# Group 0's units let in eight chain steps apart instead of six, in a fused attention and mixture-of-experts kernel

## The chip, the cores and the metric

The kernel runs on one core of a Trainium2 chip. The time is the device time of one execution in microseconds, start to end; lower is better. A core has a matmul engine (PE, with its weight loads PEld), VectorE (DVE), ScalarE (ACT), GpSimd (POOL) and SyncE (SP), each with its own queue of instructions that it works through in order, and 16 DMA engines that move data.

## What is computed

First a linear attention with a complex decay, for 4 batches, 8 heads, 768 positions and a head size of 48; then, for each of the 3072 tokens of 384 values, one of 8 experts or none.

```python
mag = sqrt(a_re**2 + a_im**2)
scale = minimum(mag, 0.999) / (mag + 1e-6)        # normalizes the decay
for t in range(768):                               # per batch and head
    S_re, S_im = a * S (complex, by row) + outer(k[t], v[t])
    y[t] = q[t] @ S_re
x = y as tokens (3072, 384)
compute = x @ w_skip > 0
e = argmax(x @ w_gate);  g = softmax(x @ w_gate)[e]
out = x + g * (relu(x @ w1[e]) @ w2[e])            # where compute, else x
```

## The kernel before

The 768 positions are six chunks of 128, taken in three groups of two chunks (NG = 3). Attention is done by chunks: inside a chunk as masked products, and across chunks by a state carried on. For this the running product of the decays is needed.

For each group five kinds of work are written as Python generators, and a small planner (class Order) mixes them into one program by estimated costs; afterwards a scheduler of the framework may move instructions within each engine's queue, so that the final order on each engine is fixed before the kernel runs.

- The chain (`chain`, L379 on) makes the running product position by position on VectorE: a step is a multiplication (L412, tile X) and an addition (L421, tile W), each needing the one before. A group has 65 steps, in eight pieces of 8 (the last of 9), and there are 195 in all; `cpos` counts them.
- The gates (`gate`, L343 on) prepare the decays of a piece for the chain: L265, L271, L272 and L275 on ScalarE, L270, L274 and L361 on VectorE.
- The consumers (`consume`, L473 on) turn a finished piece into scaled keys and queries: nw (L484) and iw (L511) on VectorE, with a sum of squares on PE (L493, tile sw) whose logarithm and exponential (L500, L501) ScalarE makes and L503 to L508 on VectorE use. For group 1 the result is written to DRAM by POOL (L533, tile kq); for groups 0 and 2 it is transposed on PE (L574).
- The units (`unit`, L640 on) are the attention of one chunk c and one batch b: eight for a group, numbered here 0 to 7 as 4 (c mod 2) + b. The names carry c and b: at_1_3 is chunk 1, batch 3, unit 7 of group 0. `unit_at` puts the products pa (L631) on PE for the next unit; the unit masks them on VectorE (L653, tile at, two halves), multiplies the carried state by the decay (L667, tile RX, from chunk 1 on), and lets PE add (L678, L679, L698, tile ps) and form the output (L709 and L712, tile py); ScalarE copies it (L714, tile yT), PE turns it (L718, tile px), and L725, L726 copy that out. The values come by DMA into one of two tiles vt (L628). Group 1's units read their keys and queries back from DRAM (L544, tile nat) and transpose them on PE (L559, tile tu).
- The router (`route`, L791 on) chooses the experts of a chunk's tokens when its four units are done: some 20 small VectorE instructions with a product on PE (L824 to L827, tile pr) between them, which L858 and L840 on VectorE read, and four scatters by POOL to the expert tables (L782, tile xs).

The units of a group are started when its last piece is consumed, while the next group's chain runs. `units` (L747 on) lets a unit in only when the chain has come far enough, by the constant PACE (L49) that the change touches. Chain 2's pieces after its first are consumed once group 0's eight units are done.

After the attention come the experts: two layers of matmuls for each, on PE, with the weights split in two parts (L993, L994), L1061 and L1088 to L1090.

Of the kernel before, what the change touches and what calls it, by code (L numbers as in the profile page):

```python
# [19 lines left out]
B, H, S, D = 4, 8, 768, 48  # L20
# [3 lines left out]
HC = 64  # L24
NCH = S // C
NG = NCH // 2
# [19 lines left out]
CREDIT = 600.0  # L46
SLACK = 0.6
AHEAD = 2
PACE = 6  # L49
FILL = 4  # L50
LATE = 6

# [60 lines left out]
class Kern:  # L113
# [633 lines left out]
    def units(self, g):  # L747
        self.nat(2 * g, 0)
        self.nat(2 * g, 1)
        self.unit_at(2 * g, 0)  # L750
        for cc in range(2):
            c = 2 * g + cc
            while self.routes_done < c - 1:
                yield 0, 200
            if c > 0:
                yield from self.make_F(c - 1)
            if not self.last(c):
                self.lg = self.rt.tile([128, B, H // 2, E + 1], F32, name=f"lg_{c}", tag="lg", bufs=2)
            self.xa = self.rt.tile([128, B, XW], F32, name=f"xa_{c}", tag="xa", bufs=2)
            self.nc.gpsimd.tensor_copy(self.xa[:, :, DM], self.tok[:, :, c])  # L760
            for b in range(B):

                while self.cpos < min((g + 1) * (HC + 1) + (cc * B + b) * PACE, NG * (HC + 1)):
                    yield 0, 100
                yield from self.unit(c, b)
                self.units_done += 1
            if not self.last(c):
                self.routes.append((self.lg_t, self.route(c, self.lg, self.xa)))
# [542 lines left out]
```

## Time and profile before

| | us |
|---|---|
| median of 3 runs | 517.73 |
| lowest and highest run | 512.75, 518.37 |
| the profiled execution | 521.83 |
| its span, first to last instruction | 520.1 |

| engine | busy us | share of the span |
|---|---|---|
| PE | 417.1 | 80% |
| DVE | 410.2 | 79% |
| ACT | 304.9 | 59% |
| POOL | 91.1 | 18% |

Busy time counts instructions at work, not waits for semaphores; a busy PE is not a PE at its peak. PE's clock has two levels, 2.4 and 1.2 GHz; the granted clock is given as a share of the upper one, 0.902 over the span. A line of the profile such as "L274 ... [4.62 <-ACT t L272]" says that the engine had been idle for 4.62 us before the instruction and that ScalarE's L272 ended this. A share of busy time is a mean over stages with different limits, so the rows below are taken by stage.

### The profile page before, as it was taken

How to read it: one execution, taken by the hardware profiler on the slowest of the kernel's cores; microseconds unless marked ns; L12 is line 12 of the kernel's file. 1: busy time of each engine (PE TensorE's matmuls, PEld its weight loads, DVE VectorE, ACT ScalarE, POOL GpSimd, SP SyncE). 2: the span in 40 equal slices, each digit the busy share in tenths (PEclk: the TensorE clock that was granted, in tenths of full speed). 3: DMA queues.
4: the chain of work that ended last, by engine and by line, in shares of the span. 5: the costliest groups of instructions: out<-in, count | busy, mean ns of one | idle time of the engine just before them, and what ended most of it. 6: DMA issues, size and time to landing. Idle time of an engine off the chain costs nothing. (4 is left out here: it accounts for less than half of the span.)

```text
span 520.1 us, 10025 instructions
## 1 busy us (share of the span) xinstructions
PE 417.1 (80%) x3253; PEld 363.1 (70%) x3253; DVE 410.2 (79%) x1119; ACT 304.9 (59%) x690; POOL 91.1 (18%) x156
## 2 busy tenths in 40 slices
PE   0346543599998422899999999999999999999994
PEld 0234322389776311787878888998999999999994
DVE  4899989998998699788988956989658678666731
ACT  5778868746464655578887663443256546554720
POOL 4002011121122355000000030212301112201111
PEclk9967668599996855699999999999999999999998
DMA  5558876799888766767745225455777777667301
GB/s 95 113 112 181 192 176 138 161 215 205 195 206 229 179 175 161 169 139 169 170 124 122 65 76 166 122 159 142 244 212 226 236 251 231 196 208 248 118 21 28
DMA packets 160370, 85.50 MB, mean 164 GB/s; under 512 B 134491, under 2 KB 154300, under 8 KB 160311
## 3 DMA queue, kind: packets, MB, share of 16 engines
q1 hardware_dynamic: 153975, 70.51, 54.1%
q0 software_dynamic: 5248, 14.07, 9.7%
q8 instruction: 28, 0.46, 0.4%
q10 hardware_dynamic: 1088, 0.20, 0.2%
q14 instruction: 31, 0.25, 0.1%
HBM read 61.62 MB, written 25.01 MB: 167 GB/s over the span
## 5 line engine op out<-in xcount | busy, mean ns | idle before, releaser
L493 PE MATMUL sw<-ws,ident 128*128 128x384 f32 x84 | 42.3, 637 | 36.0 <-ACT ws L479 35.9
L412 DVE TENSOR_TENSOR X<-W,ain 128x192 f32<-128x192 f32 x192 | 67.9, 354 | 3.7 <-ACT ain L338 0.2
L994 DVE TENSOR_TENSOR l<-r,h 128x768 fp32r<-128x768 f32 (+1 forms) x56 | 59.5, 1067 | 12.1 <-ACT h L993 11.8
L1063 ACT ACTIVATE hh<-ph 128x240 fp32r<-128x240 f32 x64 | 23.7, 374 | 57.6 <-PE ph L1061 57.6
L993 ACT CAST h<-r 128x768 fp32r<-128x768 f32 (+1 forms) x56 | 51.7, 928 | 6.8 <-DMA r<-in_moe_w_dram 5.6
L493 PEld LDWEIGHTS sw<-ws,ident 128*128 128x128 f32 x84 | 18.7, 244 | 48.3 <-ACT ws L479 38.3
L421 DVE TENSOR_TENSOR W<-X 128x96 f32<-128x96 f32 x192 | 48.9, 254 | 3.6
L1061 PE MATMUL ph<-xh,l 128*128 128x240 f32 x192 | 51.1, 275 | 0.0
L1061 PE MATMUL ph<-xh,h 128*128 128x240 f32 x192 | 49.7, 275 | 0.6 <-issue 0.6
L1061 PE MATMUL ph<-xl,h 128*128 128x240 f32 x192 | 49.3, 276 | 0.1
L581 ACT COPY qk<-tp 96x256 f32<-96x256 f32 x128 | 40.1, 370 | 12.4 <-PE tp L574 12.3
L574 PE MATMUL tp<-ident,iw 128*96 128x128 f32 x128 | 23.4, 329 | 29.7 <-DVE iw L511 24.6
L709 PE MATMUL py<-at,vt 128*64 128x128 f32 x384 | 43.7, 287 | 2.0 <-DMA vt<-in_v_dram 2.0
L1088 PE MATMUL po<-h,hh 128*120 128x384 f32 x128 | 43.4, 339 | 0.3 <-ACT hh L1063 0.3
L1089 PE MATMUL po<-l,hh 128*120 128x384 f32 x128 | 43.1, 336 | 0.0
L653 DVE TENSOR_TENSOR at<-pa,mask 128x512 f32<-128x512 f32 x48 | 32.6, 685 | 11.8 <-PE pa L631 11.3
L1090 PE MATMUL po<-h,hl 128*120 128x384 f32 x128 | 41.0, 342 | 0.0
L574 PEld LDWEIGHTS tp<-ident,iw 128*96 128x96 f32 x128 | 17.6, 153 | 33.5 <-issue 10.1
L782 POOL DMA_INDIRECT xs<-xa,sl x24 | 27.9, 1164 | 72.3 <-DVE RX L664 17.4
L1064 DVE SCALAR_TENSOR_TENSOR hl<-ph,hh 128x240 fp32r<-128x240 f32 x64 | 25.5, 403 | 16.6 <-ACT hh L1063 16.5
L631 PE MATMUL pa<-qk 96*128 96x128 f32 x256 | 35.3, 283 | 2.0 <-DVE at L653 1.7
L1061 PEld LDWEIGHTS ph<-xh,l 128*128 128x128 f32 x192 | 36.3, 189 | 0.0
(235 smaller groups left out, 1080.4 us busy)
## 6 DMA issues: line engine op xcount, KB each, us to landing
r<-in_moe_w_dram SPq DMA_DIRECT2D x24, 512.0 KB, 5.2
r<-in_moe_w_dram SPq DMA_DIRECT2D x32, 384.0 KB, 4.0
nat<-kq SPq DMA_DIRECT2D x8, 768.0 KB, 5.6
kq<-nw POOLq DMA_DIRECT2D x24, 192.0 KB, 3.6
kq<-iw POOLq DMA_DIRECT2D x24, 192.0 KB, 2.9
vt<-in_v_dram SPq DMA_DIRECT2D x24, 192.0 KB, 3.0
out_dram<-xa SPq DMA_DIRECT2D x24, 192.0 KB, 3.2
ain<-in_a_im_dram SPq DMA_DIRECT2D x90, 48.0 KB, 2.6
```

The lines of the kernel that those rows point to most:

```text
L412: V.tensor_tensor(X, prev.unsqueeze(1).to_broadcast([128, 2, 2, D]), windows(ain[:, j]), ALU.mult)
L421: self.cins = V.tensor_tensor(W[:, j, ::-1], X[:, :, 0], X[:, :, 1], ALU.add).ins
L493: nc.tensor.matmul(sw, self.ident, ws[:, :, c], start=(c == 0), stop=(c == 1))
L574: nc.tensor.transpose(tp[:, jj], src[:, s * 4 + jj], self.ident)
L581: nc.scalar.copy(o, tp[:, :, :, cc].rearrange("p j s b -> p b s j"))
L709: PE.matmul(py[j * 64:j * 64 + 64, hp], vt_[:, 2 * hp + j], at[:, 2 * hp + j], start=True, stop=(c == 0))
L993: nc.scalar.copy(hi[:, ks], raw)
L994: nc.vector.tensor_tensor(lo[:, ks], raw, hi[:, ks], ALU.subtract)
L1061: pe = PE.matmul(ph, w[:, k, js], x[:, k], start=(n == 0), stop=(n == len(terms) - 1))
L1088: PE.matmul(po, hh[:, j, sl], w2h[:, j], start=(j == 0), stop=False)
L1089: PE.matmul(po, hh[:, j, sl], w2l[:, j], start=False, stop=False)
L1090: pe = PE.matmul(po, hl[:, j, sl], w2h[:, j], start=False, stop=(j == NF - 1))
```

## The change

PACE was one number, 6, and is now a number for each group, 8 for group 0 and 6 for groups 1 and 2. Unit n of group g may be written once the chain's count is at 65 (g + 1) + n PACE, at most 195. For group 0 that was 65, 71, 77, ... 107 and is 65, 73, 81, ... 121. Groups 1 and 2 keep 130, 136, ... 172 and 195.

```diff
-PACE = 6
+PACE = (8, 6, 6)
@@ units
-                while self.cpos < min((g + 1) * (HC + 1) + (cc * B + b) * PACE, NG * (HC + 1)):
+                while self.cpos < min((g + 1) * (HC + 1) + (cc * B + b) * PACE[g], NG * (HC + 1)):
                     yield 0, 100
                 yield from self.unit(c, b)
```

What this does to the queues is seen in three places. In VectorE's queue the masks of group 0's eight units stood behind 76, 78, 81, 85, 90, 97, 101 and 107 chain steps, and now stand behind 76, 78, 82, 89, 97, 105, 113 and 121.

The first place is PE's queue around the product of group 0's first route, pr_0 (tri and ones are constants of the count, oh the chosen experts). Before:

```order
L718 MATMUL px_1_1_1637<-wg_100,yT_1_1_1635 128x105 x4
L709 MATMUL py_1_2_1754<-at_1_2_1719,vt0_162 64x128 x2
L698 MATMUL ps_1_2_1740<-vt0_162,nat_1_2_1544 96x48 x8
L712 MATMUL py_1_2_1754<-qk_0_1_201,st0_164 64x128 x2
L709 MATMUL py_1_2_1754<-at_1_2_1719,vt0_162 64x128 x2
L712 MATMUL py_1_2_1754<-qk_0_1_201,st0_164 64x128 x2
L709 MATMUL py_1_2_1754<-at_1_2_1719,vt0_162 64x128
L824 LDWEIGHTS tri_75
L824 MATMUL pr_0_1707<-oh_0_1672,tri_75 128x32
```

The same queue in the changed kernel, up to the same product:

```order
L718 MATMUL px_1_0_1625<-wg_100,yT_1_0_1623 128x105 x4
L631 MATMUL pa_1_2_0_1728<-qk_0_1_201 128x128 x4
L709 MATMUL py_1_1_1752<-at_1_1_1706,vt1_163 64x128 x2
L824 LDWEIGHTS tri_75
L824 MATMUL pr_0_1685<-oh_0_1662,tri_75 128x32
```

The product stood behind five of the pieces of unit 6 (py_1_2, ps_1_2), and now stands behind one half of unit 6's pa and the first two products of unit 5.

The second place is ScalarE's queue around L271 and L272 of gate 15, the last gate of group 1 (t_15 is what VectorE's L274 reads). Before:

```order
L705 COPY T_1_3_1895<-ps_1_3_1883 96x384
L479 ACTIVATE ws_13_1960<-W_13_1860 128x768
L714 COPY yT_1_3_1914<-py_1_3_1897 128x512
L271 ACTIVATE sq_15_1943<-sq_15_1943,col_80 128x432
L272 ACTIVATE t_15_1944,acc_108<-sq_15_1943,col_80 128x432
```

In the changed kernel:

```order
L681 COPY st1_165<-ps_1_1_1738 96x8x48
L705 COPY T_1_1_1750<-ps_1_1_1738 96x384
L271 ACTIVATE sq_15_1827<-sq_15_1827,col_80 128x432
L714 COPY yT_1_1_1769<-py_1_1_1752 128x512
L272 ACTIVATE t_15_1828,acc_108<-sq_15_1827,col_80 128x432
```

The copy in front of L272 was unit 7's and is now unit 5's. VectorE's L274 of gate 15 stood behind chain step 115 and unit 7's RX behind 108; now L274 stands behind 113 and unit 5's RX behind 106.

The third place is POOL's queue at the end of group 1, with the stores of its last piece (nw_15, iw_15) and the scatters of group 0's second route (xa_1). Before:

```order
L782 DMA xs_117<-xa_1_1454,sl_1_2104 2048x386
L760 COPY xa_2_2341<-tok_98 128x4
L533 DMA kq1_119<-nw_15_2170 64x8x96
L533 DMA kq1_119<-nw_15_2170 64x768
L782 DMA xs_117<-xa_1_1454,sl_1_2104 2048x386 x2
L533 DMA kq1_119<-iw_15_2204 64x768
L533 DMA kq1_119<-iw_15_2204 64x8x96
L782 DMA xs_117<-xa_1_1454,sl_1_2104 2048x386
```

In the changed kernel:

```order
L533 DMA kq1_119<-nw_15_2115 64x8x96
L533 DMA kq1_119<-nw_15_2115 64x768
L533 DMA kq1_119<-iw_15_2189 64x768
L533 DMA kq1_119<-iw_15_2189 64x8x96
L782 DMA xs_117<-xa_1_1504,sl_1_2207 2048x386 x4
```

Three of the four scatters stood ahead of the last two stores, and now all four stand behind them. On VectorE the first small instruction of that second route (L802) stood behind chain step 118 and now stands behind 132; L511 of the last piece stood behind 135 and now behind 136; and the first mask of group 1 stood behind 146 and now behind 149.

## Rows read from the trace of the kernel before

**Rows 1.** Windows: length, busy us (x instructions) of PE, PEld, DVE, ACT, POOL, clock, DMA.

```profile
113.50:157.90 44.40, 41.13 (x361) 33.85 (x360) 41.75 (x113) 25.77 (x60) 9.67 (x17) 1.00 0.91 208
157.90:174.60 16.70, 16.70 (x125) 13.26 (x124) 9.80 (x31) 7.24 (x16) 4.80 (x7) 0.69 0.87 219
174.60:196.00 21.40, 3.90 (x14) 1.72 (x12) 21.02 (x73) 12.46 (x29) 9.31 (x16) 0.61 0.67 163
220.50:302.70 82.20, 82.20 (x715) 66.59 (x715) 71.17 (x191) 62.40 (x151) 2.41 (x5) 1.00 0.57 130
302.70:520.10 217.40, 207.55 (x1758) 200.47 (x1758) 147.01 (x405) 99.80 (x203) 39.10 (x41) 0.99 0.56 171
```

**Rows 2.** The same view for two stretches at the lower clock.

```profile
158.80:169.10 10.30, 10.30 (x60) 7.95 (x59) 8.09 (x27) 2.83 (x7) 2.41 (x4) 0.50 0.88 223
213.40:220.30 6.90, 6.90 (x40) 6.79 (x39) 3.90 (x8) 4.66 (x9) 0.00 (x0) 0.51 0.58 108
```

**Rows 3.** VectorE's waits, 100 to 225 us: us in total, times, longest.

```profile
DVE sq L274 <- ACT t L272: 4.6, 1, 4.6
...
DVE ohs L858 <- PE pr L825: 2.0, 1, 2.0
```

**Rows 4.** Timeline: start us, us, engine, line, operation, tiles, [idle before <-releaser].

```profile
157.76 0.44 PE L709 MATMUL py<-at,vt 128*64 128x128 f32 x4 [1.55 <-DMA vt<-in_v_dram]
...
162.18 0.21 PE L824 MATMUL pr<-oh,tri 128*128 128x32 bf16 x1
...
162.45 0.17 DVE L858 TENSOR_TENSOR ohs<-ohs,cnt 128x8 bf16<-128x8 bf16 x1 [2.04 <-PE pr L825]
...
172.61 0.59 ACT L714 COPY yT<-py 128x512 f32<-128x512 f32 x1 [0.54 <-PE py L712]
...
174.57 0.61 DVE L274 SCALAR_TENSOR_TENSOR sq<-sq,t 128x432 f32<-128x432 f32 x1 [4.62 <-ACT t L272]
```

**Rows 5.** Timeline at the start of group 1's units.

```profile
200.13 2.84 POOL L782 DMA_INDIRECT xs<-xa,sl  x1 [2.75 <-DMA xs<-xa,sl]
...
200.87 0.95 DVE L511 TENSOR_TENSOR iw<-inv,W 128x768 f32<-128x768 f32 x1
...
202.95 1.31 POOL L533 DMA_DIRECT2D kq<-iw  x2
...
213.06 1.57 PE L559 MATMUL tu<-ident,nat 128*96 128x128 f32 x8 [0.78 <-DMA nat<-kq]
...
220.49 0.69 DVE L653 TENSOR_TENSOR at<-pa,mask 128x512 f32<-128x512 f32 x1 [3.15 <-PE pa L631]
```

**Rows 6.** Lines, 113.5 to 157.9 us, DVE then PE: count | busy us, mean ns | idle.

```profile
L653 DVE TENSOR_TENSOR at<-pa,mask 128x512 f32<-128x512 f32 x12 | 8.0, 683 | 0.5 <-PE pa L631 0.5
L421 DVE TENSOR_TENSOR W<-X 128x96 f32<-128x96 f32 x29 | 7.4, 255 | 0.6
...
L667 DVE TENSOR_TENSOR RX<-T,F 96x768 f32<-96x768 f32 x4 | 3.8, 947 | 0.0
...
L631 PE MATMUL pa<-qk 96*128 96x128 f32 x90 | 12.1, 282 | 0.8 <-DVE at L653 0.7
L698 PE MATMUL ps<-vt,nat 128*96 128x48 f32 x80 | 7.6, 245 | 0.0
L709 PE MATMUL py<-at,vt 128*64 128x128 f32 x83 | 7.3, 279 | 2.0 <-DMA vt<-in_v_dram 2.0
L718 PE MATMUL px<-wg,yT 128*128 128x105 f32 x48 | 6.4, 276 | 0.3 <-ACT yT L714 0.3
L493 PE MATMUL sw<-ws,ident 128*128 128x384 f32 x16 | 6.1, 505 | 0.1
L712 PE MATMUL py<-qk,st 96*64 96x128 f32 x32 | 3.2, 278 | 0.0
L678 PE MATMUL ps<-RX,ident 96*96 96x384 f32 x6 | 2.5, 498 | 0.0
L679 PE MATMUL ps<-RX,perm 96*96 96x384 f32 x6 | 2.4, 485 | 0.0
```

## The prediction

> **What bounds the kernel now.** I read three things, in this order: where the time lies by stage, which engine is full in each, and what the full engine waits for. The stages come from the windows of busy time [rows 1]. From 220.5 us on the matmul engine is full: 82.20 us busy of 82.20 while group 1's units run, and 207.55 of 217.40 from there to the end, for group 2's units and the experts. Whatever makes the stretch from 220.5 us begin earlier moves the end by the same amount, since the PE queue after it holds the same work. Before it, VectorE sets the pace: it is busy 41.75 us of 44.40 while group 1's chain and six of group 0's units run together, and 21.02 of 21.40 at the end of that chain. Between the two lies the stretch to look at, 157.9 to 174.6 us: VectorE is busy 9.80 us of 16.70. That is the tail of group 0's units, and the change touches exactly these.
>
> The waits of VectorE between 100 and 225 us [rows 3] name what it stood for: 4.6 us for ScalarE's `t`, and 2.0 us for the router's PE product `pr`. The timeline [rows 4] shows how the first two came about. PE idled 1.55 us for `vt` and began again at 157.76; from 158.8 to 169.1 us its granted clock was 0.50, the lower of its two levels, 1.2 GHz [rows 2]. Units 6 and 7 (the last two of group 0's eight, counted from 0) stand close behind each other in PE's queue, so everything behind them was late: `pr` at 162.18 behind the products of unit 6, for which L858 waited 2.04 us, and unit 7's `py`, for whose copy `yT` at 172.61 ScalarE waited with the gate's L271 and L272 behind it, so that VectorE's L274 began only at 174.57, 4.62 us late. The chain's own steps stand behind L858 and L274 on VectorE and waited too.
>
> **The change, part by part.** No instruction is added or removed but for the grouping of a few; units move. By VectorE's order the masks of units 2 to 7, which stood behind chain steps 81, 85, 90, 97, 101 and 107, now stand behind 82, 89, 97, 105, 113 and 121. Units 0 and 1 stay at 76 and 78, because they are admitted late.
>
> *Router's product.* PE's order has `pr` behind unit 6's `pa` and unit 5's first two products instead of behind half of unit 6's `py`. Its wait, 2.0 us, goes: -2.0.
>
> *Gate's chain on ScalarE.* The copy that stands in front of L272 of gate 15 is now unit 5's, whose multiplication RX is issued seven chain steps earlier than L274, not unit 7's. -4.6.
>
> *What is late next.* Does a unit fit between two masks eight steps apart? VectorE first: in 44.4 us it did 29 steps, and in the same stretch 8.0 us of masks and 3.8 us of RX [rows 6]; without these (44.4 - 11.8) / 29 = 1.12 us a step with the gates and consumption it carries, so eight steps and one unit (2 x 0.683 + 0.947 = 2.3) take 9.0 + 2.3 = 11.3 us. PE: one unit of the second chunk has 16 records of L631, L698, L709 and L712, 8 of L718, 2 each of L678 and L679, and 4 of the consumption's L493. By busy time over count [rows 6] that is 2.15 + 1.52 + 1.41 + 1.60 + 1.07 + 0.83 + 0.80 + 1.53 = 10.9 us; these lines overlap (47.6 us summed against 41.13 as a union), so 10.9 x 0.864 = 9.4 us. It fits at 2.4 GHz with 1.9 us to spare, and not at 1.2 GHz, where it would take 18.8. One low stretch like that of [rows 2], 10.3 us, loses 5.15 us of PE work; 1.9 are spare, so up to 3.3 us reach VectorE. With the four units of the second chunk the new waits lie between 0 and 4 x 3.3 = 13.2 us. I take 2.0, about the smaller of the two old waits once, since PE is no longer queued two units deep and the masks, the consumption's products and RX are in PE's order in the order in which VectorE needs them: +2.0.
>
> *Start of group 1.* Its units read `nat` from DRAM, which needs the last stores `kq<-iw` of chunk 15. Before, POOL's queue has three of the four scatters of the second route ahead of these: L511 began at 200.87 and ended near 201.8, but the stores were issued at 202.95, when the scatter of 200.13 was through its 2.84 us [rows 5]. Now all four scatters stand behind the stores: -1.1. The second route itself moves from step 118 to step 132; its last six small instructions move behind L511, but one chain step more stands before it, so L511 sees no difference that I can price. PE's first product of group 1 waited for `nat` until 213.06 and VectorE's first mask for PE until 220.49 [rows 5], so it is `nat` that starts the full stretch. The mask's 3.15 us of waiting is PE's lateness seen from VectorE and is not counted a second time: the order puts three chain steps more ahead of that mask, which uses the time without making PE earlier. From 213.4 to 220.3 PE ran at 0.51 [rows 2]; if that goes, half of 6.9 us, 3.4, is gained; I leave it where it is, since PE still idles between unit 7 and group 1.
>
> *What hides nothing more.* The gates, loads and consumption that move with the units lie beside VectorE's chain as before. DMA engines are at 0.91 busy while the units run six apart [rows 1]; spreading them cannot raise that.
>
> **Sum.** -2.0 - 4.6 - 1.1 + 2.0 = -5.7 us. The profiled execution took 521.83 us in all (span 520.1), which makes 516.1. The median of the three runs is 517.73, 0.8% under the profiled one; against it the same difference makes 512.0.
>
> The trace has PE's clock at 0.61 where the units have ended and PE has 3.90 us of work in 21.40, at 1.00 over the 44.4 us in which units stand six apart [rows 1], and falling right after an idle of 1.55 us [rows 2, 4]; by these rows a spacing of eight with 9.4 us of work in 11.3 lies nearer to the second, and the sum stays 516.1. The Trainium skill, page "TensorE: Matmul & The Clock Gate", section "HAM oscillation — how this bites in real kernels", says that a matmul engine whose short bursts are parted by waits is throttled again in every round. By that rule spreading the units is the wrong direction and every unit of the second chunk would run low, which gives 523.2. The trace agrees with it at 158.8 us and no run shown here has the spacing of eight. As a mechanism of this kernel it is the second rival below.
>
> **Rivals.**
> 1. *The waits come back elsewhere.* In two of the four spacings the clock falls and VectorE waits 3.3 us at L503 or L274: -7.7 + 6.6 = -1.1, 516.6. For it: L503 stands only three to four steps behind the mask that its product L493 follows on PE. Against: at 2.4 GHz that path fits.
> 2. *Slower: every unit of the second chunk runs low.* The place is PE between masks 97 and 121. Price 4 x 3.3 = 13.2 against 7.7: +5.5, 523.2. It decides from the third low spacing on (9.9 against 7.7). For it: 1.9 us of idle per spacing could lie in one piece, and an idle of 1.55 was enough once. Against: a low PE is full, and PE rose again after a full stretch.
> 3. *More than forecast.* No new wait, and group 1 starts at 2.4 GHz: -7.7 - 3.4 = -11.1, 506.6.
> 4. *The change does nothing.* Excluded by the order: six of eight units move.
>
> **How the numbers follow.** Forecast 0.45, rival 1 0.33, rival 2 0.12, rival 3 0.10. The predicted time is the forecast's, 512.0. The range reaches down to rival 3, 506.6, and up to three low spacings, -7.7 + 9.9 = +2.2, 519.9; beyond it stay rival 2's full price and a little below. About 1%, 5.2 us, is what a measurement of this kernel can tell from no change. The forecast lies just beyond it: most of its share and all of rival 3 are faster, the rest of it and rival 1 lie within, and of rival 2 most is slower. That makes 0.48, 0.41, 0.11.
>
> **What would show it.** Right: in the profile of the changed kernel VectorE's waits at L858 and at gate 15's L274 are gone, no wait of over 2 us stands between masks 3 and 7, the store of chunk 15's `iw` follows L511 at once, the masks of group 1 begin some 5 us earlier, and everything from there is shifted alike. Wrong: a granted clock of 0.5 through most of the second chunk's units with waits at L503, L274 or L653, or a stretch from group 1's first product to chain 2's end longer than before by what was won.

## The result, and the profile after

The changed kernel is slower, by little: 519.0 us (median of 20 executions, 517.27 to 523.05) against 516.83 us of before (20 executions on the same chip, 512.75 to 519.95). The ratio is 1.0055, with a 95% interval from 1.0034 to 1.0077. The forecast was 512.0 us. The time lies in the range that was given (506.6 to 519.9), near its upper end, and on the other side of no change.

The profiled execution of the changed kernel took 519.52 us (span 517.8), so it is 2.3 us *shorter* than the profiled one of before (521.83 us), while the median is 2.2 us longer. That is the first thing to see: one execution beside one execution gives the wrong sign here.

| | before | changed |
|---|---|---|
| median of 20, us | 516.83 | 519.0 |
| shortest of 20, us | 512.75 | 517.27 |
| profiled execution, us | 521.83 | 519.52 |
| its span, us | 520.1 | 517.8 |
| its granted clock, mean | 0.90 | 0.91 |

Windows of busy time of the changed kernel, as in [rows 1, 2]: length, then busy us (instructions) of PE, PEld, DVE, ACT and POOL, then granted clock, DMA share and GB/s.

```profile
113.50:157.90 44.40, 36.65 (x308) 30.29 (x307) 41.62 (x120) 25.54 (x56) 10.24 (x18) 0.96 0.87 212
157.90:174.60 16.70, 13.51 (x127) 10.35 (x125) 15.83 (x40) 8.96 (x20) 7.04 (x11) 1.00 0.88 212
174.60:198.60 24.00, 12.10 (x79) 9.35 (x79) 21.86 (x78) 14.33 (x34) 6.38 (x11) 0.73 0.79 184
211.10:216.40 5.30, 5.29 (x17) 3.68 (x18) 3.85 (x10) 2.38 (x4) 0.97 (x1) 0.50 1.00 193
306.70:517.80 211.10, 201.34 (x1710) 195.40 (x1708) 144.51 (x399) 94.59 (x189) 38.77 (x39) 0.99 0.56 173
```

The stretch from 157.9 to 174.6 us, in which VectorE was busy 9.80 us before [rows 1], now has 15.83 us of VectorE work, and TensorE's clock is at its upper level in it. The last units have moved on into the end of the chain (12.10 us of PE work in the 24.0 us from 174.6 us on, where before had 3.90 in 21.4).

VectorE's waits in the changed kernel, 100 to 225 us: us in total, times, longest. They answer to [rows 3].

```profile
DVE ws L503 <- ACT ws L501: 3.4, 4, 1.8
DVE at L653 <- PE pa L631: 1.2, 2, 0.8
DVE RX L667 <- PE ps L679: 1.2, 1, 1.2
DVE sq L274 <- ACT t L272: 1.0, 2, 0.8
```

The wait at L858 is gone, and the wait at L274 has shrunk from 4.6 to 1.0 us. No wait is longer than 1.8 us.

The start of group 1 in the changed kernel, answering to [rows 5]: start us, us, engine, line, operation, tiles, [idle before <-releaser].

```profile
198.58 0.95 DVE L511 TENSOR_TENSOR iw<-inv,W 128x768 f32<-128x768 f32 x1
...
199.82 1.23 POOL L533 DMA_DIRECT2D kq<-iw  x2 [9.00 <-DVE X L412]
...
205.33 1.50 SPq L544 DMA_DIRECT2D nat<-kq  x2
...
210.23 0.95 DVE L667 TENSOR_TENSOR RX<-T,F 96x768 f32<-96x768 f32 x1
...
211.11 1.91 PE L559 MATMUL tu<-ident,nat 128*96 128x128 f32 x8 [4.71 <-DMA nat<-kq]
...
212.81 1.49 PE L678 MATMUL ps<-RX,ident 96*96 96x384 f32 x2
...
217.85 0.69 DVE L653 TENSOR_TENSOR at<-pa,mask 128x512 f32<-128x512 f32 x1 [0.38 <-PE pa L631]
```

Two things differ from before. TensorE stood idle for 4.71 us in one piece ahead of its first turn (L559), where before it waited 0.78 us. And the two products of RX (L678, L679) come behind the turn; in before they came ahead of it, with a wait of 1.00 us of their own:

```profile
210.75 0.89 PE L678 MATMUL ps<-RX,ident 96*96 96x384 f32 x2 [1.00 <-DVE RX L667]
```

From 211.10 to 216.40 us, the first of group 1's work, the clock of the changed kernel is 0.50. The profiled execution of before had 0.51 there too [rows 2].

### The profile page after: what moved, and what is told of

Same layout as the page of the kernel before. It is cut to its first block, busy times and chain, and to the rows that moved or that the text cites. A ratio compares the mean times of both kernels' runs of the same rounds, so it can differ in the third digit from the quotient of the medians.

```text
span 517.8 us, 10027 instructions
## 1 busy us (share of the span) xinstructions
PE 416.8 (80%) x3253; PEld 362.2 (70%) x3253; DVE 409.9 (79%) x1119; ACT 305.2 (59%) x690; POOL 90.4 (17%) x156
## 5 line engine op out<-in xcount | busy, mean ns | idle before, releaser
L493 PE MATMUL sw<-ws,ident 128*128 128x384 f32 x84 | 44.8, 662 | 31.8 <-ACT ws L479 31.8
L709 PE MATMUL py<-at,vt 128*64 128x128 f32 x384 | 42.1, 288 | 0.0
L631 PEld LDWEIGHTS pa<-qk 96*128 96x128 f32 x256 | 31.9, 194 | 8.4 <-issue 3.2
## 6 DMA issues: line engine op xcount, KB each, us to landing
r<-in_moe_w_dram SPq DMA_DIRECT2D x24, 512.0 KB, 5.1
```

What stands on the lines that cost most here:

```text
L493: nc.tensor.matmul(sw, self.ident, ws[:, :, c], start=(c == 0), stop=(c == 1))
L631: nc.tensor.matmul(pa[h // 4][:, h % 4], KT(h), QT(h), start=True, stop=True)
L709: PE.matmul(py[j * 64:j * 64 + 64, hp], vt_[:, 2 * hp + j], at[:, 2 * hp + j], start=True, stop=(c == 0))
```

## The experiments

### Were the waits typical of before?

No line of the kernel is changed in the next three: before twice more, and the changed kernel once more. The fourth asks for a spacing in between.

```
p7:  -PACE = (8, 6, 6)
     +PACE = (7, 6, 6)
```

> The kernel before, unchanged, profiled a second time. Theory A (the first profile of before was an untypical execution: the 2.0 us wait at L858 and the 4.6 us wait at L274 follow from a low clock at 158.8 us that most executions don't have): the two waits sum to under 3 us here, the span is near 515, and the chain's steps 80 to 130 take 73 to 75 us against 79.6 in the first profile. Theory B (the waits are always there and the change loses its gain later, in group 1's or 2's units): both waits are there again, 6 us and more in sum, and steps 80 to 130 take 79 to 80 us. Timed against itself: a ratio of 1.000 within its interval by both.

> The kernel before, unchanged, a third profile. Theory A: as in the second, the two waits under 3 us in sum and steps 80 to 130 in 73 to 75 us. Theory B: 6 us of waits and 79 to 80 us.

> The changed kernel (8, 6, 6) again. By both theories some 0.5% slower than before in time (519 us). Theory A: steps 80 to 130 take 71 to 74 us as in its first profile (71.8), hardly less than before typically takes, and 2 to 3 us are lost from step 130 to the first product of group 1 or in group 1's units. Theory B: steps 80 to 130 some 7 us shorter than before's, and all of it lost after step 130.

> Group 0's units seven steps apart (7, 6, 6). Theory A: the distance has little to win, so the time lies between the two or near before, 516 to 519 us. Theory B: half of the waits go and half of the later loss comes: 516 to 519 as well; they differ in where: A has steps 80 to 130 within 2 us of before's typical execution, B has them 3 to 4 us shorter.

Measured: before 519.61 us (median of 10), against itself a ratio of 1.0005 [0.9963, 1.0047], and 523.11 us (one execution); the changed kernel 520.02 us, ratio 1.0043 [0.9997, 1.0088]; seven apart 520.53 us, ratio 1.0045 [1.0004, 1.0085], above the 516 to 519 us that both theories gave it. VectorE's waits in the second profile of before, 100 to 225 us:

```profile
DVE at L653 <- PE pa L631: 4.5, 2, 3.4
DVE ws L503 <- ACT ws L501: 1.4, 3, 0.8
DVE ain L361 <- ACT t L275: 1.1, 1, 1.1
DVE sq L274 <- ACT t L272: 0.9, 2, 0.5
```

The same program, and neither of the two waits on which the forecast rested: L858 is not in the list, and L274 waits 0.9 us instead of 4.6. In the third profile L858 is not in the list either, and L274 has:

```profile
DVE sq L274 <- ACT t L272: 1.2, 1, 1.2
```

Chain steps 80 to 130 took 73.0 us in the second profile, about what theory A expected, and 77.1 us in the third, between the two theories. The busy times show more than the waits do. Below is one window from the end of chain step 80 to the end of the last iw (L511) of group 1, in the three profiles of before and the changed kernel's two.

Before, first profile:

```profile
113.52:201.82 88.30, 61.88 (x494) 48.81 (x492) 78.34 (x235) 48.43 (x108) 26.53 (x41) 0.81 0.83 196
```

Before, second profile:

```profile
117.17:198.88 81.71, 56.24 (x487) 44.49 (x485) 78.17 (x236) 48.19 (x108) 25.61 (x41) 0.85 0.88 208
```

Before, third profile:

```profile
113.88:199.69 85.81, 61.32 (x493) 49.38 (x491) 78.45 (x235) 49.01 (x108) 27.19 (x41) 0.80 0.85 202
```

Changed kernel, first profile:

```profile
115.89:199.53 83.64, 59.87 (x489) 47.60 (x487) 77.95 (x232) 48.35 (x108) 22.72 (x38) 0.90 0.84 202
```

Changed kernel, second profile:

```profile
117.99:200.56 82.57, 59.68 (x487) 46.43 (x485) 78.05 (x232) 48.22 (x108) 22.72 (x38) 0.89 0.85 203
```

Read the third figure, VectorE's busy time: 78.34, 78.17, 78.45, 77.95, 78.05 us. The work is the same whatever the spacing, and only the idle time (length less busy) differs: 9.96, 3.54, 7.36 us in before, 5.69 and 4.52 us in the changed kernel. Up to step 80 the queues of the two kernels are alike, so what differs there is the execution alone. The forecast wanted to take 6.6 us of two waits out of before; in its other two profiles these two sum to 0.9 and 1.2 us.

### Is VectorE full to the end of the chain?

The last 17 products X of group 1's chain are issued twice (the same values are written again), once in before and once in the changed kernel.

```
-                    V.tensor_tensor(X, prev..., windows(ain[:, j]), ALU.mult)
+                    for _ in range(2 if g == 1 and 48 <= p * LP + j < 65 else 1): V.tensor_tensor(X, prev..., windows(ain[:, j]), ALU.mult)
```

> Before, with each of the last 17 products X of group 1's chain (steps 114 to 130) issued twice on VectorE: the same values are written again, and no other work is changed. One such product took 0.353 us in the profiles of before, so VectorE gets 6.0 us more work in that stretch. Theory V: from step 80 to the last iw of chain 1 (L511) VectorE is full in a usual execution of before (3.5 us of idle in 81.8 us in the second profile of before), and the stretch is as long as VectorE's work. It then costs 5 to 6 us: 523 to 525 against the 518.5 of before. Theory S, on which the forecast rested: the end of chain 1 has several us of slack on VectorE in before. It then costs 0 to 1.5 us: 518.5 to 520.

> The same doubled products in the changed kernel. Theory V: the changed kernel has as much VectorE work up to the last iw as before (77.8 to 78.2 us against 78.2 to 78.5), only laid out otherwise, and no more slack or less at the end of the chain: 5 to 6 us more, 525 to 526 against its 519.5, and the same step as in before. Theory S: the units now fill the slack, so here the full 6 us show while before shows 0 to 1.5.

Measured: in before 523.11 us against 517.19, ratio 1.0129 [1.0076, 1.0183], 5.9 us for 6.0 us of work. So there was no slack at the end of the chain to spread units into; theory V holds and S falls. In the changed kernel 522.21 us, ratio to before 1.0112 [1.0058, 1.0166]; taken against its own 1.0055 that is about 2.9 us, half of what V expected, a miss. The window from step 80 to the last iw, before with doubled products:

```profile
115.97:207.26 91.29, 59.41 (x491) 48.24 (x489) 84.56 (x253) 49.00 (x108) 27.08 (x43) 0.79 0.82 191
```

The same window of the changed kernel with them:

```profile
117.31:204.87 87.56, 59.28 (x482) 45.70 (x480) 82.93 (x241) 48.77 (x108) 22.89 (x38) 0.88 0.83 195
```

In the changed kernel 4.9 of the 6.0 us lie ahead of the last iw (82.93 less 78.0), the idle time is 4.63 us as without them, and the first turn came 11.0 us after the last L511 began instead of 12.5. The two doublings are not quite alike, since other rows moved in the queues with them: in the changed kernel the products of RX, which began 1.7 us behind the first turn, now begin 4.7 us behind it (219.64 against 214.92 us). Why not more of the 6.0 us reaches the end was not settled.

### Four apart, ten apart, and the change at group 1

```
p4:    PACE = (4, 6, 6)
p10:   PACE = (10, 6, 6)
p686:  PACE = (6, 8, 6)
```

> The first number is 4: group 0's units stand four steps apart, the opposite of the change. Theory V: VectorE's work up to the last iw of chain 1 stays the same 78 us, so the distance does not matter by itself: 517 to 521, and VectorE idle between step 80 and the last iw of 3 to 7 us. Theory S: the end of the chain is then still emptier, and the waits ahead of it grow: 522 to 527. If the wider spacing itself costs something, as the 0.55% of the change suggest, four apart should be faster than six: 514 to 517.

> The first number is 10: seven spacings of 10 steps are more than the 65 steps of the chain, so that the last unit of group 0 begins after chain 1's end. Theory V: the last iw comes earlier by that unit's VectorE work (about 4 us), and the unit is paid in group 1's stretch where TensorE is full: within 517 to 522. If the spacing itself costs, in proportion: 520 to 523. If the start of group 1 (low clock, the wait for nat) is what costs in the changed kernel, the unit's products fill that wait: 515 to 518.

> The numbers (6, 8, 6): the change is made for group 1 alone, group 0 stays as before. In group 1 TensorE is full and its units lag the gate (in before the last unit's mask begins at 309 us, and step 186 of the chain, at which it would be let in, ends at 279 us), so that the gate holds nothing back. Theory V (the distance matters only through waits): 517 to 519.5, the same as before. If a wider spacing costs wherever it is put: 520 to 523.

Measured: four apart 517.66 us, 0.9985 [0.9941, 1.003], the same as before within that interval; a spacing narrower by two neither gains nor loses. The change at group 1 alone 519.81 us, 1.0025 [0.9982, 1.0068], no difference that can be measured. But this says nothing of a wider spacing: in the profile of (6, 8, 6) every engine has the same instructions in the same order as in before's. The gate holds nothing back in group 1, so this is before's program once more. Ten apart 529.01 us, 1.0261 [1.0195, 1.0328], worse than every expectation for it. The window from group 1's first turn to the start of its last unit's mask, ten apart:

```profile
212.57:314.45 101.88, 100.63 (x844) 81.19 (x845) 81.17 (x230) 74.62 (x186) 8.16 (x12) 0.97 0.55 129
```

It has 33 records (instructions) of PE more than the 811 of the same stretch of before (213.06 to 309.74 us), since products of group 0's last unit now lie where TensorE is full; TensorE is busy 100.63 us there instead of 96.17. That is about 4.5 us of the 12; the rest was not followed up. The unit did not fill the wait for nat (2.1 us are left of it), and the last iw did not come earlier (86.94 us behind step 80).

The profile of (6, 8, 6), a fourth one of before's program, met the L274 wait again:

```profile
DVE sq L274 <- ACT t L272: 4.8, 1, 4.8
```

So the wait is real, but it comes in some executions only: in two of the four profiles of before's program. Eleven profiles, with those of kernels further down, have before's chain 1; in the other nine no single wait of L274 is over 1.6 us, and the wait of L858 is in the first profile alone.

### The start of group 1

The changed kernel never showed a time below 517 us: 0 of 30 executions in its two series. Before was below 517 us in 49 of 156 (all its series, two executions of over 800 us left out). Four apart was profiled in such a short execution (515.93 us). First 5 us from group 1's first turn, and the window from there to the start of the last unit's mask, four apart:

```profile
212.91:217.91 5.00, 5.00 (x44) 4.60 (x45) 4.47 (x10) 3.26 (x6) 0.00 (x0) 1.00 0.99 186
212.91:304.29 91.38, 91.06 (x803) 75.60 (x804) 77.67 (x205) 71.30 (x174) 2.40 (x5) 1.00 0.59 132
```

The same two windows of the changed kernel:

```profile
211.11:216.11 5.00, 5.00 (x16) 3.39 (x17) 3.54 (x10) 2.38 (x4) 0.97 (x1) 0.50 1.02 198
211.11:306.68 95.57, 95.30 (x807) 77.76 (x808) 77.67 (x206) 72.91 (x175) 5.93 (x9) 0.97 0.57 130
```

With the clock at 1.00 TensorE gets through 44 records in its first 5 us, with 0.50 through 16, and the whole stretch is 4.2 us shorter. This led to theory T1: the changed kernel loses at the start of group 1, where TensorE now idles in one piece. Two ways to test it: fill the idle time with work of no use (12 transposes of the identity into the turn's own buffer, which the turn then overwrites), or shorten it (the second transfer of nat issued behind the first turn).

```
warm_a: behind the line that makes tp in turn:
+  [nc.tensor.transpose(tp[:, 0]..., self.ident[:, 0:96], self.ident) for _ in range(12 if (c, b, hh, q) == (2, 0, 0, 0) else 0)]

nl_a, nl_b:
-        self.nat(2 * g, 1)
         self.unit_at(2 * g, 0)
+        if self.spilled(g): self.nat(2 * g, 1); self.behind(self.nat_ins, [self.tu_ins])
```

> The changed kernel, with 12 transposes of the identity on TensorE put ahead of group 1's first turn (into the product's own buffer, which the turn then overwrites), where TensorE sits idle for 4.7 to 4.9 us until nat has landed; nothing else is changed. Theory T1: the changed kernel loses its gain at the start of group 1, because after that one long idle stretch TensorE runs its first 5 us there at the low clock in every execution (low until 216.4 in both of its profiles, 95.3 to 95.6 us from the first turn to the last mask of group 1, against 91.4 us in the profile of the 4-apart kernel, whose clock was up by then). The transposes fill the idle stretch, the clock is up when the turns begin, that stretch takes 91 to 93 us, and the median is 515.5 to 517.5. Theory T2: the loss is somewhere else, in chain 1 or later. The transposes then change nothing, or cost up to 1 us where nat lands earlier: 519 to 521.

> The same in the changed kernel, where TensorE waits 4.7 to 4.9 us for nat in one piece. The first nat should land 2 to 2.5 us earlier and the first turn begin at 208.5 to 209. Theory T1 (start of group 1 and its clock): a gain of 2 to 2.5 us and perhaps the clock too, 515.5 to 517.5. Theory T2: the products of group 1 then wait for VectorE at the first masks instead, and 519 to 520 stays.

> Before, with the second transfer of nat for group 1 issued behind the first turn on TensorE, some seven loads later on SP, so that the first one has the DMA engines to itself; the first is 768 KB of 1536 KB that now land together 5.6 to 6.2 us after their issue. It tests whether the start of group 1's full stretch sets the end one to one. In before TensorE waits 0.8 to 1.1 us for the first nat: the start moves by that much at most, 517 to 518.5 against 518. If the landing of nat isn't what holds the start: 518 to 519.

Measured: with the 12 transposes the changed kernel takes 516.85 us (512.02 to 518.83) against 519.11 of before, ratio 0.9957 [0.9928, 0.9986]. Work of no use turned a loss into a gain. Its timeline at the place:

```profile
203.75 1.52 PE L557 MATMUL tu<-ident 128*96 128x128 f32 x12 [1.14 <-ACT qk L581]
...
206.33 1.08 PE L559 MATMUL tu<-ident,nat 128*96 128x128 f32 x8 [1.06 <-DMA nat<-kq]
...
207.37 0.89 PE L678 MATMUL ps<-RX,ident 96*96 96x384 f32 x2
```

Its windows ahead of the transposes, from them to the turn, of the turn's first 5 us, and from the turn to the start of the last unit's mask:

```profile
200.00:203.75 3.75, 2.62 (x10) 1.63 (x8) 3.37 (x10) 3.25 (x10) 1.00 (x1) 0.61 0.65 130
203.75:206.33 2.58, 1.52 (x13) 1.27 (x13) 2.58 (x8) 1.54 (x4) 0.00 (x0) 1.00 1.18 308
206.33:211.33 5.00, 5.00 (x31) 3.85 (x32) 4.81 (x11) 3.31 (x6) 0.97 (x1) 1.00 1.07 207
206.33:299.70 93.37, 92.86 (x807) 75.85 (x808) 77.78 (x206) 72.52 (x175) 6.09 (x9) 1.00 0.59 133
```

In this profile the transposes do not raise the clock, they keep it up. It has come up behind the products of sw and tp, as it does in the changed kernel too, whose windows over the same place follow:

```profile
201.85:206.40 4.55, 4.54 (x12) 2.80 (x12) 4.09 (x13) 2.91 (x7) 2.02 (x2) 0.52 0.71 159
206.40:209.60 3.20, 0.00 (x0) 0.00 (x0) 3.18 (x9) 2.75 (x8) 0.00 (x0) 1.00 0.98 240
209.60:216.40 6.80, 5.29 (x17) 3.70 (x18) 5.34 (x12) 2.38 (x4) 0.97 (x1) 0.50 1.04 216
```

There it stands at 1.00 from 206.40 to 209.60 us while TensorE has nothing to do, and is down again when the turn comes. In the second profile of the changed kernel with transposes (warm_a2 below) the clock was still at 0.50 while they ran, from 207.54 us on, and came up just behind them, with 0.93 over the turn's first 5 us.

The other test gave nothing. In before the wait for nat stayed at 0.9 us, so the second transfer isn't what makes the first one late; 520.99 us, 1.0022 [0.9979, 1.0066], where a small gain was expected. In the changed kernel the wait shrank to 3.4 us in one piece and the time stayed at 521.25 us, 1.002 [0.9975, 1.0064]. Its first 5 us ran at 0.52, and here the clock had not come up ahead of the turn at all: it was 0.50 from 179.2 to 215.2 us. A miss for T1's second number: the shorter idle stretch did not help.

### The order alone, and both kernels with the same start

These kernels part the order from the spacing. cool_b is before with one thing of the changed kernel: TensorE takes the first turn ahead of the products of RX. Some later rows of the queues of TensorE, VectorE and ScalarE stand elsewhere too, all from that place on; with the transposes it is the same. cw_b has the 12 transposes in addition, warm_a2 is the changed kernel with them once more, and warm_b puts 24 products of the identity into sw's buffer ahead of the first sw of chain 2.

```
cool_b:
-                PE.matmul(ps, self.ident[0:96, 0:96], X[:, 0], start=True, stop=False)
+                x = PE.matmul(ps, self.ident[0:96, 0:96], X[:, 0], start=True, stop=False).ins; _ = self.behind(x, [self.tu_ins]) if (c, b) == (2, 0) else None

warm_b: behind the line that makes sw in consume:
+  [nc.tensor.matmul(sw[:, 0:2]..., self.ident, self.ident[:, 0:96], start=True, stop=True) for _ in range(24 if i == 2 * NP else 0)]
```

> Before, with one thing of the changed kernel alone: at the start of group 1 TensorE takes the first turn (which waits for nat) ahead of the two products of RX, as it does in the changed kernel; in before it takes them behind. Nothing of the spacing is changed. Theory T1 (the changed kernel loses its gain by the idle TensorE ahead of the first turn): TensorE idles 4 to 5 us there, the low clock always reaches into group 1, and the times below 516 that before shows in about three of ten executions are gone: median 1 to 2 us above that of before, none below 516. Theory T2 (this order costs nothing, the loss lies in the spacing): the same as before within 0.2%.

> The same order, and 12 transposes of the identity in the idle stretch ahead of the first turn, as in the changed kernel that had them (516.85, 0.43% below before). So before and the changed kernel meet group 1 alike, and only the spacing differs. If the spacing itself brings nothing once the starts are alike: the same as that kernel, 516 to 518. If chain 1 does gain by the spacing (1 us on the mean of the profiles, 83.1 against 84.1 us from step 80 to the last iw): 1 to 2 us more than it, 517.5 to 519. If the spacing costs: 514 to 516.

> The changed kernel with the 12 transposes once more, beside the two kernels above and in more rounds. Theory T1: 516 to 517.5, faster than before by 0.3 to 0.6%, and the range of its times narrower than that of before. If its first result was chance: within 0.2% of before.

> Before with 24 products of the identity in the 8.9 us in which TensorE idles ahead of the first sw of chain 2 (into sw's own buffer, which is then overwritten), with the products of RX still ahead of the first turn. Theory T1: the clock comes up before the first turn in more executions than in before, so that more of its times lie below 517: 516 to 517.5. Theory T2: the same as before, or up to 1 us more where the products make sw late.

Measured, all against 518.79 us of before on that chip:

| kernel | spacing | start of group 1 | median us | ratio [95%] |
|---|---|---|---|---|
| cool_b | 6 | turn first | 520.66 | 1.0058 [1.0015, 1.0101] |
| cw_b | 6 | turn first, 12 transposes | 515.73 | 0.9964 [0.9935, 0.9994] |
| warm_a2 | 8 | turn first, 12 transposes | 516.50 | 0.9962 [0.9928, 0.9996] |
| warm_b | 6 | as before, 24 products earlier | 522.42 | 1.0084 [1.0051, 1.0117] |

The turned order alone gives 1.0058, where the whole change gave 1.0055, and none of cool_b's 12 executions is below 517 us (lowest 517.54). With the same start, six apart and eight apart have the same time (0.9964 and 0.9962): the spacing itself is worth nothing that can be measured here, where each ratio is known to some 0.3%, 1.6 us. Timeline of cool_b at the start of group 1:

```profile
206.09 0.95 DVE L667 TENSOR_TENSOR RX<-T,F 96x768 f32<-96x768 f32 x1
...
208.72 1.91 PE L559 MATMUL tu<-ident,nat 128*96 128x128 f32 x8 [2.61 <-DMA nat<-kq]
...
210.42 1.49 PE L678 MATMUL ps<-RX,ident 96*96 96x384 f32 x2
```

Its windows ahead of the turn, of the turn's first 5 us and from the turn to the start of the last unit's mask:

```profile
187.00:208.70 21.70, 5.29 (x14) 3.01 (x15) 20.80 (x64) 12.50 (x29) 8.97 (x12) 0.50 0.83 196
208.72:213.72 5.00, 5.00 (x16) 3.39 (x17) 3.65 (x8) 3.60 (x8) 0.00 (x0) 0.50 1.00 180
208.72:305.39 96.67, 95.77 (x815) 78.56 (x816) 80.53 (x210) 74.10 (x179) 3.98 (x7) 0.97 0.56 127
```

The idle stretch is 2.61 us here, less than the 4 to 5 that were expected, and the clock is at its lower level behind it as in the changed kernel. But it did not fall in this stretch: it was 0.50 from 187.0 us on. The same windows of cw_b, which differs by the transposes:

```profile
213.84:218.84 5.00, 5.00 (x41) 4.33 (x42) 4.52 (x10) 4.29 (x10) 0.00 (x0) 1.00 0.94 172
213.84:307.44 93.60, 93.04 (x815) 76.95 (x816) 78.98 (x209) 73.20 (x179) 4.74 (x8) 1.00 0.58 131
```

warm_b missed its aim. Its 24 products ran from 184.15 to 189.75 us, ahead of another product that waits, and the 9.1 us of idle time ahead of sw stayed; its first 5 us of group 1 ran at 0.50. It is slower, which T1 did not expect of it, and why was not followed up.

### The transposes alone

```
w12_b:  before, with the line of the 12 transposes alone
cw_b2:  the kernel of cw_b once more
```

> Before with the 12 transposes of the identity alone, and its own order kept: they stand behind the transposes tp of iw's piece and ahead of the products of RX and the first turn, where TensorE in before idles in two pieces of about 1 us each (for RX, then for nat). Theory T1: what counts is that TensorE does not stand idle ahead of group 1. The idle time here is only about 2 us, so the transposes (2.4 to 4.8 us) delay the turn by 0.5 to 2.5 us, and in return the clock is up in more executions: 516 to 518, 0 to 0.4% faster than before. If the order of the turn counts and not the idle time: no better than before, 518.5 to 520.5.

> Six apart, the turn ahead of the products of RX, and the 12 transposes, once more, as the version to keep: 0.2 to 0.6% faster than before, 516 to 517.

Measured: 515.97 us against 518.75, 0.9953 [0.9916, 0.9989]; and 516.46 us, 0.9987 [0.9958, 1.0017]. So the transposes help with before's own order too, and the second measurement of cw_b is not clear by itself. The versions that beat both kernels are before or the changed kernel with 12 transposes ahead of group 1's first turn, by 0.4 to 0.5% against before (0.9953, 0.9957, 0.9962, each interval below 1). First 5 us and stretch of w12_b:

```profile
208.26:213.26 5.00, 5.00 (x44) 4.52 (x45) 4.62 (x9) 4.29 (x10) 0.00 (x0) 1.00 1.00 180
208.26:302.52 94.26, 93.56 (x811) 76.50 (x812) 78.18 (x206) 73.06 (x178) 4.96 (x7) 1.00 0.58 130
```

All profiles together (ten apart, which has part of another unit in the stretch, and warm_b left out): the clock in the first 5 us from group 1's first turn, and the us from there to the start of the last unit's mask and to the end of the span.

| order at the start of group 1 | clock, one figure for each profile | us to the mask | us to the end |
|---|---|---|---|
| as before, no transposes (8 profiles) | 0.54 0.50 0.50 0.81 1.00 0.91 1.00 0.71 | 96.7 97.0 96.7 94.4 93.6 93.9 91.4 92.8 | 307.1 308.4 310.9 304.7 304.8 304.3 301.2 303.8 |
| turn first, no transposes (5) | 0.50 0.54 0.52 0.50 0.67 | 95.6 95.2 95.3 96.7 95.7 | 306.7 307.0 307.6 307.0 306.9 |
| 12 transposes (5) | 1.00 0.93 1.00 1.00 1.00 | 93.4 93.5 93.6 93.7 94.3 | 304.0 303.8 303.9 304.7 304.7 |

Before's order meets group 1 at 0.71 or more in five of eight profiles, the turned order in none of five, and with the transposes all five do. The first four of the eight are before's own program, and of these only one does. The stretch to the mask takes 95.2 to 97.0 us at 0.50 to 0.67 and 91.4 to 94.4 at 0.71 to 1.00, which is some 2.5 us between the groups: what 5 us at half the clock lose. To the end it is 306.7 to 310.9 against 301.2 to 304.8 us, 3.7 us between the means; where the 1.2 us beyond the 2.5 come from was not seen. Before's program alone shows both: 304.7 us at 0.81, and 307.1 to 310.9 at 0.50 and 0.54. At the lower clock the turned order takes no longer than that (306.7 to 307.6 us).

The mean granted clock of every execution is on record as well. Over the executions that the ratios use it is 0.900 in cool_b against 0.905 in before, which makes some 5.6 us more at the lower level (an estimate, give or take 4), and in w12_b 0.910 against 0.905, some 4.9 us less (give or take 4.5). That is about the 5 us of the table. In the changed kernel it is 0.903, as in before: its clock is higher from step 80 to the last iw, where VectorE paces (0.90 and 0.89 against 0.80 to 0.85), so that the mean alone does not show the start of group 1.

## Why the prediction was wrong, step by step

**What bounds the kernel.** Right. In before VectorE paces up to the last iw (5.9 us for 6.0 us more work), and TensorE after group 1's first turn: in the profiled pair the first mask of group 1 comes 2.6 us earlier and the span ends 2.3 us earlier.

**The step that failed first: the base.** The terms -2.0 (the router's product) and -4.6 (the gate's chain) were read from one execution, and the sum was made against that one. In the profiles the mechanism did what was said: the two waits are gone from the changed kernel, and the idle time of VectorE from step 80 on went from 9.96 to 5.69 us, 4.3 less. But over eleven profiles with before's chain 1 the idle time is 3.3 to 10.0 us, 5.9 on average, and over six with the changed chain 1 it is 4.4 to 8.9, 5.4 on average. The two waits, priced at 6.6 us, sum to some 2.3 us on the mean of the eleven and to some 0.8 on that of the six. Against the mean idle time, the 6.6 us were worth about 0.5, and with this spread between profiles that is known to some 2 us only. A warning stood in the prediction itself: the profiled execution was 0.8% above the median of the three runs, which is 4.1 us, more than half of the sum. Taking the difference of one execution over to a median that is 4 us lower carried over waits that most of the eleven profiles do not have.

**What is late next, +2.0.** About right: the changed kernel waits 3.4 us at L503 and 1.0 at L274, where the second profile of before waits 1.4 and 0.9, so 2.1 us more (the second profile of the changed kernel has 3.1 and 0.2, 1.0 more); and no wait of over 2 us stands between masks 3 and 7, as was said.

**POOL, -1.1.** The store does follow L511 at once now (L511 ends at 199.53, the store is issued at 199.82), as foreseen. But in the second profile of before it does too (198.88 and 199.18): the scatter's 2.84 us in [rows 5] were again that execution's. And the first turn came 12.5 us after L511 began, 12.2 in before: nothing gained.

**The start of group 1, 0: the step that made it a loss.** The prediction saw 6.9 us at the lower clock there [rows 2], called 3.4 us of it a possible gain, and left it "where it is, since PE still idles between unit 7 and group 1". It did not ask what TensorE's queue has at that place. In the changed kernel RX lies further back (its start is 11.7 us behind that of the last L511, 8.9 in before, with the next piece's L503 to L511 now ahead of it), the turn stands ahead of RX's products, and the two short pauses of before (1.0 and 0.8 us) become one of 4.71. cool_b shows that this order alone costs 1.0058, as much as the change. By the table this goes with the clock: at the lower level the turned order takes no longer to the end than before's, and the upper level is worth 3.7 us. If before met it in five of eight executions, the turned order would lose some 2.3 us (an estimate) by never meeting it; cool_b's 3 us have an interval from 0.8 to 5.2. The weak point is that share, which comes from eight profiles of five programs; that the shortest times are gone (0 of 30 executions below 517 us, where before has 49 of 156) speaks for it. Two results stay open. Seven apart keeps before's order there, with 0.71 in its profile, and is at 1.0045 [1.0004, 1.0085] all the same, and warm_b keeps it too and is at 1.0084; so a further cost beside this order is not excluded.

**The rivals.** The slower case was there, but with another mechanism: every unit of the second chunk at the low clock. That did not happen; the clock is 0.96 and 1.00 from 113.5 to 174.6 us, and 0.50 in short stretches only (141.3 to 144.7 and, under part of the last unit, 182.3 to 189.1 us). The Trainium skill, page "TensorE: Matmul & The Clock Gate", section "HAM oscillation — how this bites in real kernels", says that where a burst is shorter than the wait behind it, the next one starts throttled again. For units eight steps apart the trace does not agree; for group 1's first turn in the changed kernel, behind 4.71 us of nothing, it does, with 0.50. So the rule held at the one place where the prediction did not apply it. Rival 1 (the waits come back elsewhere, -1.1) came nearest to what chain 1 did.

**What would show it.** The masks of group 1 were to begin 5 us earlier. In the profiled pair it is 2.6 (217.85 against 220.49), and the stretch behind, from the first turn to the last unit's mask, takes 95.6 and 96.7 us, since both profiles met the low clock there. The sign of being wrong, a stretch from group 1's first product to chain 2's end that is longer by what was won, did not show either: it takes 88.3 us (211.11 to 299.38) against 89.6 in before (213.06 to 302.68). One pair could not show the loss, because this profile of before had lost the upper clock too; with before's order the stretch to the mask takes 91.4 to 94.4 us where the clock was up.

## What to carry to other kernels

Before a wait is priced, look at how the profiled execution stands to the median: if it is longer by about as much as the waits that are to go, they may be its own, and a second profile, or the busy time of the engine that paces the stretch (here 78 us in every profile), tells more than a list of waits. Spreading work out beside a full engine can gain no more than that engine's idle time, as long as its own work stays the same; so count the idle time first, over more than one profile. And where a reordering changes what an engine does just ahead of a stretch in which it is full, read its queue there: an idle piece in front of the stretch can cost as much as the waits that the reordering removes. Before a variant is taken as a test, compare its queues with those of the kernel that it varies: (6, 8, 6) was the same program.

## What the hardware showed that was not expected

- Executions of one program on one core, taken on several chips, spread by 2.8% (512.75 to 527.19 us over 156 executions), and which waits VectorE meets changes with them; up to chain step 80, where the two kernels' queues are alike, the profiles already differ by up to 5 us (113.0 to 118.0 us).
- Twelve transposes of no use, 1.5 us of TensorE's time, shorten the kernel by 0.4 to 0.5%. With them the clock is 0.93 to 1.00 over the first 5 us of group 1 in five of five profiles; in the changed kernel without them, behind an idle stretch of 4.7 us, it is 0.50.
- The granted clock stood at 1.00 for 3.2 us in which TensorE did nothing (206.40 to 209.60 in the changed kernel) and at 0.50 when the work came: it follows what the engine did earlier.
